# First chunk of a spectral block: the last two tiles' rows placed on chip, the rest read in one transfer, four banks for the first transforms, weight splits spread over three engines

## The chip, the cores and the metric

The kernel runs on one core of a Trainium2 chip. The metric is the device time of one execution in microseconds, here the median of several runs. A core has five engines with queues of their own: TensorE (matmuls and their weight loads), VectorE, ScalarE, GpSimd and SyncE, which here only issues transfers. Each works in program order and waits on semaphores; transfers issued by SyncE, ScalarE or GpSimd run on 16 DMA engines that they share.

## The reference, cut to what matters

The input x has 4096 rows of 640 channels.

```python
mod = (silu(c) @ w_mod).reshape(1, 6, 1, 640)      # sa, ca, ga, sb, cb, gb
h = layernorm(x) * (1 + ca) + sa
x = x + ga * A(h, w1, b1, w2, b2)
h = layernorm(x) * (1 + cb) + sb
x = x + gb * ((silu(h @ w_gate) * (h @ w_up)) @ w_down)
# A: rfft over the 4096 rows; 4 channel blocks of 160; a complex two-layer
# perceptron per frequency (w1, relu, w2); soft shrink by 0.01; inverse rfft
```

All of it is float32 in and out. Where matmuls run on the chip's rounded float32 type, an operand is split into a rounded high part and the remainder, the low part, and the products are summed.

## The kernel before, in words

The 4096 rows are seen as 128 x 32 (n1, n2). **Stage A** (lines 420 to 434) works on eight tiles t, each with four values of n2: `xas[t]` holds 128 partitions (n1) x 4 x 640 channels. Per tile: statistics on VectorE and GpSimd (`ln_stats`), normalisation in place on ScalarE and VectorE (`ln_apply`, L387 and L389), a transform over n1 by five matmul blocks (`dft_a`, L407), and the evacuation of the five banks into the same tile (`evac_a`, L414 to L418). Block i of 0 to 3 takes 128 of 160 channels of each group from row i; block 4 takes the remaining 32 of each group from all four rows (the remainder block). After it, partitions are frequencies. Their order is fixed by the constant `fa`: partition m belongs to a chunk `ch` (0 to 7), and within it to q (4) and jj (4).

The result must be turned so that n2 lies on partitions. It goes through a scratch in device memory, `s1`, in three families: f0 (chunks 0 and 1, every fourth partition, 320 KB per tile), f1 (chunks 2 and 3, 320 KB) and f2 (chunks 4 to 7, every second partition, 640 KB). `write_s1(t, f)` (L338) writes a tile's rows; `load_g(ch)` (L307) reads a chunk into `g`, a tile of 128 partitions (n2, q) x 4 x 640, by four transfers, one for each q. `g` has two buffers. `moves(t)` (L348) is what SyncE issues after tile t: the f0 write always, inputs of later stages, from t=4 f1 and f2 writes of tiles 1 to 3; at t=6 GpSimd is given the read of chunk 0 for n2 below 28, and at t=7 SyncE issues the last four n2, four reads of 40 KB. SyncE's queue then holds the read of chunk 1, `tb` of chunk 1, `b2t`, the f1 writes of tiles 0 and 4 to 7, the read of chunk 2, and the f2 writes of the same tiles (L443 to L453).

**Weights** (`prep_weights`, L253): w1 is split into w1a, w1b and w1c by twelve jobs on ScalarE (high, L280) and VectorE (low, L283) after stage A; w2 into w2a, w2b and w2c by six jobs on GpSimd (high, L278) and VectorE (low).

**Middle stage** (loop at L768): p counts the 32 pairs of chunk and channel group (ch, b), p = 4 ch + b. Its steps: `stage_b` (L542), the transform over n2 into a bank `pb`, and its evacuation, on ScalarE and VectorE, `evac_b` (z, L549 and L550) and `evac_r` (rz, L572 and L582); `stage_l1` (layer 1, L603 to L621, banks p1 and p3), `tail_l1`, `stage_l2` (layer 2, L649, banks p2, evacuated into `tt` on VectorE at L651), `move_x` (tt to `xx` on chip, SyncE, L665), `shrink`, `stage_i` (inverse over n2, L702 to L706, written to the scratch s2 by GpSimd). The order within one p is written out by hand; layer 2 runs one p behind layer 1, `stage_b` one chunk ahead. `stage_b` uses bank b0, or b1 for the remainder block (t=4), one of each. Before the loop, blocks 0, 4, 1 and 2 of chunk 0 are transformed and evacuated, and three low splits of w2 are made; the other three come at the end of p=0. `mods` and `sums` spread the loads and sums of w_mod over the loop; their buffer `wm` (L477) is single, a load waits for the sum before.

After the loop the last chunk's inverse, the first rows of the second normalisation, and then the feed-forward part, from about 330 us to the end.

Memory: the eight tiles `xas` (10,240 bytes per partition each) are released by `stx.close()`, and the pool `p2` takes their place. A tile of p2 may be written once every reader of the tile that lay there is done, scratch writes included. From the allocation: w2a, w2b and w2c lie on xa1, xa2 and xa3, `tt` on xa4, acc, cl, wx and bx on xa0, xx from xa5 on.

Of the kernel before, what the change touches and what calls it, by code (L numbers as in the profile page):

```python
# [6 lines left out]
F32 = mybir.dt.float32  # L7
# [39 lines left out]
def constants():  # L47
# [9 lines left out]
    for ch in range(8):  # L57
        for p in range(2):
            for ri in range(2):
                for jj in range(4):  # L60
                    r = 4 * (2 * p + ri) + jj
                    m = 4 * (16 * (ch % 2) + r) + (0, 2, 1, 3)[ch // 2]
# [109 lines left out]
def body(tc, x, w1, b1, w2, b2, wg, wu, wd, c, wm, k_fa, k_tb, k_tx, k_bm, k_bx, k_ga, k_ge, k_id, out, dbg=None):  # L172
# [9 lines left out]
    s1 = [nc.dram_tensor(f"s1{f}", (n, N2, D), F32, kind="Internal").ap() for f, n in enumerate((32, 32, 64))]  # L182
# [17 lines left out]
    with ExitStack() as top:  # L200
# [33 lines left out]
        with ExitStack() as af:  # L234
# [50 lines left out]

            af.enter_context(tc.manual_schedule())
# [12 lines left out]
            def load_g(ch, lo=0, hi=32, dma=None):  # L299
                if ch < 4:  # L300
                    src = s1[ch // 2].rearrange("(c q j) n d -> c q n j d", c=2, q=4)[ch % 2]
                else:
                    src = s1[2].rearrange("(c q j f) n d -> f c q n j d", c=2, q=4, f=2)[ch // 2 - 2, ch % 2]
                if lo == 0:
                    gs[ch] = fx.tile([P, 4, D], F32, tag="gx", bufs=2, name=f"g{ch}")
                for q in range(4):
                    (dma or nc.sync).dma_start(gs[ch][4 * lo + q:4 * hi:4], src[q, lo:hi])  # L307
# [16 lines left out]
            with tc.tile_pool(name="sp", bufs=1) as sp:  # L324
# [23 lines left out]
                def moves(t):  # L348
                    write_s1(t, 0)
                    if t == 0:  # L350
                        load_x(6)
                        nc.sync.dma_start(c5, c)
                    elif t == 1:
                        load_x(7)
                        raws[1] = load_weights(sp, w1, "1")
                    elif t == 2:
                        nc.sync.dma_start(wm1, wm[:, 1])
                    elif t == 3:
                        load_tb(0)
                        nc.sync.dma_start(b1m, b1[:, 0:8].rearrange("p (r b) -> p r b", r=2))  # L360
                        nc.sync.dma_start(b1r, b1[0:64, 8:12])
                        raws[2] = load_weights(rp, w2, "2")
                    elif t < 7:
                        if t == 6:
                            load_g(0, 0, 28, pool)
                        for f in (1, 2):
                            write_s1(t - 3, f)
                    else:
                        load_g(0, 28, 32)
# [30 lines left out]
                def dft_a(t):  # L400

                    xnr = xas[t].rearrange("p a (b e) -> p a b e", b=NB)
                    for i in range(5):
                        j = 5 * t + i
                        pa = (bank0(j // 4, [P, 512], f"pa{t}_{i}") if j % 4 == 0
                              else ps.tile([P, 512], F32, tag=f"p{j % 4}", name=f"pa{t}_{i}"))
                        mm(pa, fa, xnr[:, i, :, 0:128] if i < 4 else xnr[:, :, :, 128:160], start=True, stop=True)  # L407
                        pas[t, i] = pa

                def evac_a(t):  # L410
                    xa = xas[t]
                    for i in range(5):
# [10 lines left out]
                for t in range(8):  # L423
                    if t + 2 < 8:
                        ln_stats(t + 2)
                    if t + 1 < 8:
                        ln_apply(t + 1)
                    dft_a(t)
                    if t == 7:
                        first_scale()  # L430
                    evac_a(t)
                    if t == 2:
                        act.activation(sc, c5, AF.Silu)
                    moves(t)
# [4 lines left out]
                for job in prep_weights(raws[1], w1a, w1b, w1c, True):  # L439
                    weights_high(*job)  # L440
                    weights_low(*job)

            hp = af.enter_context(tc.tile_pool(name="hp", bufs=1, reuse_waits="tile"))  # L443
            load_g(1)
            load_tb(1)
            b2t = hp.tile([P, 2, NB, BS], F32, name="b2t")
            nc.sync.dma_start(b2t, b2.rearrange("r b o -> (r b o)").partition_broadcast(P))
            for t in (0, 4, 5, 6, 7):
                write_s1(t, 1)
            load_g(2)  # L450
            load_tb(2)
            for t in (0, 4, 5, 6, 7):
                write_s1(t, 2)  # L453
# [4 lines left out]
            pool.dma_start(bm.rearrange("p a b c -> p (a b c)"), k_bm)  # L458
            p2 = af.enter_context(tc.tile_pool(name="p2", bufs=1, side="right", reuse_waits="tile"))

            acc = p2.tile([P, D], F32, name="acc")
            cl = p2.tile([P, D], F32, name="cl")
            wx = p2.tile([P, P], F32, name="wx")
            bx = p2.tile([P, 2, 128], F32, name="bx")
            w2a = p2.tile([P, NB, 640], F32R, name="w2a")
            w2b = p2.tile([P, NB, 640], F32R, name="w2b")
            w2c = p2.tile([P, NB, 640], F32R, name="w2c")
            prep2 = prep_weights(raws[2], w2a, w2b, w2c, False)
            for job in prep2:
# [6 lines left out]
            def mod_load(m, k):  # L476
                wmts[m, k] = p2.tile([P, D], F32, tag="wm", bufs=1, name=f"wm{m}_{k}")  # L477
# [59 lines left out]
            def stage_b(ch, t):  # L537
                g, tb = gs[ch], tbs[ch]
                pb = bank0(1 if t == 4 else 0, [P, 2, 256], f"pb{ch}_{t}")
# [228 lines left out]
            for p in range(LAST + 1):  # L768
# [20 lines left out]
                on(stage_l2, p - 1)  # L789
# [4 lines left out]
                if b == 0 and ch:  # L794
                    for i in range(4):
                        move_x(ch - 1, i)
                if p == 0:
                    for job in prep2[3:]:
                        weights_low(*job)
# [12 lines left out]
            def load_first():  # L812
                x2 = fx.tile([P, 4, D], F32, tag="gx", bufs=2, name="x2_0")
                nc.sync.dma_start(x2, xv[:, 0:4, :])
# [6 lines left out]
            for p in range(LAST + 1, NP):  # L821
# [6 lines left out]
                elif p == LAST + 2:  # L828
                    load_first()
# [3 lines left out]
                on(shrink_low, p - 5)  # L833
            on(shrink, LAST - 1)
# [49 lines left out]
            def first_norm(i):  # L884
                mv, rs, nm = fst[i]
                xn = p2.tile([P, D], F32, tag="co" if i < 2 else "wm", bufs=2 if i < 2 else 1, name=f"xn0_{i}")
# [348 lines left out]
```

## Time and profile before

| | us |
|---|---|
| median of 3 runs (1500.94 to 1502.04) | 1501.2 |
| the profiled execution, its own time | 1502.37 |
| its span, first to last instruction | 1500.6 |
| TensorE busy | 1456.5 (97%) |
| VectorE, ScalarE, GpSimd busy | 871.8, 587.7, 117.0 |
| TensorE busy in 0 to 20, 20 to 40, 40 to 60, 60 to 80, 80 to 100 us | 11.54, 18.09, 10.41, 13.26, 17.50 |

The profile names an instruction by its source line, its engine, and the tiles that it writes and reads (out<-in); for each group it gives the busy time and the idle time just before it, with what ended that idle time. A row like "SPq" or "POOLq" is the queue that issues transfers. "Landing" is when a transfer's last byte is confirmed. The chain of waits runs back from the last instruction of the execution: at each step to what released it, or to the instruction before it.

### The profile page before, as it was taken

What the parts mean: (1) busy time and instruction counts of PE and PEld (TensorE: products, weight loads), DVE (VectorE), ACT (ScalarE), POOL (GpSimd) and SP (SyncE); (2) the same over time, 40 slices, a digit from 0 to 9 for tenths busy, and PEclk for the clock granted to TensorE, in tenths of its full rate; (3) what the DMA queues carried; (4) which work ended last, traced back from release to release, by engine and by line L of the source; (5) the groups of instructions that cost most, each with busy time, mean ns of one, the idle gap of its engine ahead of it and who ended that gap; (6) DMA issues with size and microseconds to landing.
All of it is one profiled execution on the core that took longest, in us unless ns stands there. A gap on an engine that the chain in (4) does not pass through costs nothing.

```text
span 1500.6 us, 20793 instructions
## 1 busy us (share of the span) xinstructions
PE 1456.5 (97%) x8114; PEld 1292.2 (86%) x8114; DVE 871.8 (58%) x1598; ACT 587.7 (39%) x1034; POOL 117.0 (8%) x215
## 2 busy tenths in 40 slices
PE   7599999989999999999999999999999999999998
PEld 2399999868989898989898989898889988898888
DVE  8478888877475437543844374447444744564433
ACT  7569989746232314231323132313231322223220
POOL 5400100030010001000100010001000100000000
PEclk9799999999999999999999999999999999999999
DMA  9946556647432423241324132513241324223210
GB/s 377 319 168 188 167 160 184 206 135 233 140 88 84 111 74 97 85 138 47 100 84 138 53 102 75 154 36 102 80 140 53 94 80 131 62 71 89 70 44 35
DMA packets 183057, 179.92 MB, mean 120 GB/s; under 512 B 19312, under 2 KB 153648, under 8 KB 180016
## 3 DMA queue, kind: packets, MB, share of 16 engines
q1 hardware_dynamic: 173728, 152.56, 34.0%
q0 software_dynamic: 3904, 14.91, 3.0%
q10 hardware_dynamic: 5328, 11.14, 2.0%
q8 instruction: 63, 1.03, 0.3%
q14 instruction: 34, 0.28, 0.1%
HBM read 137.95 MB, written 31.46 MB: 113 GB/s over the span
## 4 chain that ended last, share of the span: by engine, by line
PE 84%; DVE 5%; ACT 4%; DMA 4%; POOL 1%; SPq 1%; issue 1%; DVEq 0%; ACTq 0%; POOLq 0%
PE pd L1143 26%; PE pg L1050 8%; PE pg L1049 8%; PE pg L1051 8%; PE pu L1050 8%; PE pu L1049 8%; PE pu L1051 8%; PE pc L649 1%; PE pl L603 1%; PE pa L407 1%; DMA xx<-tt 1%; PE pb L542 1%; PE pt L1031 1%; DMA s<-xa 1%; DMA g<-s 1%
## 5 line engine op out<-in xcount | busy, mean ns | idle before, releaser
L1143 PE MATMUL pd<-wdh,ah 128*128 128x320 f32 x1664 | 384.4, 310 | 0.1
L1143 PEld LDWEIGHTS pd<-wdh,ah 128*128 128x128 f32 x1664 | 282.4, 188 | 1.0 <-DVE yo L1147 0.4
L1143 PE MATMUL pd<-wdl,ah 128*128 128x320 f32 x832 | 257.0, 309 | 0.0
L1044 DVE TENSOR_TENSOR wl<-wr,wh 128x640 fp32r<-128x640 f32 x216 | 177.5, 822 | 121.5 <-ACT wh L1043 121.5
L1050 PE MATMUL pg<-ht,wh 128*128 128x512 f32 x555 | 216.2, 389 | 0.0
L1049 PE MATMUL pg<-ht,wh 128*128 128x512 f32 x555 | 216.1, 389 | 0.0
L1051 PE MATMUL pg<-ht,wl 128*128 128x512 f32 x555 | 216.0, 389 | 0.0
L1049 PE MATMUL pu<-ht,wh 128*128 128x512 f32 x515 | 200.8, 390 | 0.0
L1050 PE MATMUL pu<-ht,wh 128*128 128x512 f32 x515 | 200.6, 390 | 0.0
L1051 PE MATMUL pu<-ht,wl 128*128 128x512 f32 x515 | 200.4, 389 | 0.0
L1107 ACT ACTIVATE sg<-pg 128x512 f32<-128x512 f32 x104 | 62.2, 598 | 336.2 <-PE pg L1051 335.3
L1120 ACT ACTIVATE ah<-sg 128x512 fp32r<-128x512 f32 x104 | 65.8, 632 | 295.4 <-DVE sg L1119 295.4
L1043 ACT ACTIVATE wh<-wr 128x640 fp32r<-128x640 f32 x216 | 157.1, 728 | 41.5 <-DVE x L1148 38.2
L1147 DVE TENSOR_TENSOR yo<-pd,gbb 128x320 f32<-128x320 f32 x128 | 62.7, 490 | 183.7 <-PE pd L1143 183.7
L1143 PEld LDWEIGHTS pd<-wdl,ah 128*128 128x128 f32 x832 | 156.3, 188 | 0.6
L1051 PEld LDWEIGHTS pg<-ht,wl 128*128 128x128 f32 x555 | 104.2, 188 | 21.8
L1119 DVE TENSOR_TENSOR sg<-pu,sg 128x512 f32<-128x512 f32 x104 | 71.7, 689 | 88.1 <-PE pu L1051 88.1
L1049 PEld LDWEIGHTS pg<-ht,wh 128*128 128x128 f32 x555 | 104.2, 188 | 21.0
L1050 PEld LDWEIGHTS pg<-ht,wh 128*128 128x128 f32 x555 | 104.2, 188 | 21.0
L1121 DVE TENSOR_TENSOR ah<-sg,ah 128x512 fp32r<-128x512 f32 x104 | 72.2, 694 | 72.7 <-ACT ah L1120 72.7
L1051 PEld LDWEIGHTS pu<-ht,wl 128*128 128x128 f32 x515 | 96.7, 188 | 20.3
L1049 PEld LDWEIGHTS pu<-ht,wh 128*128 128x128 f32 x515 | 96.7, 188 | 19.6
(209 smaller groups left out, 2001.6 us busy)
## 6 DMA issues: line engine op xcount, KB each, us to landing
wr<-in_B_w_gate_dram SPq DMA_DIRECT2D x104, 320.0 KB, 3.3
wr<-in_B_w_up_dram SPq DMA_DIRECT2D x104, 320.0 KB, 3.2
x<-in_A_x_dram SPq DMA_DIRECT2D x8, 1280.0 KB, 6.2
out_dram<-x ACTq DMA_DIRECT2D x31, 320.0 KB, 2.2
g<-s SPq DMA_DIRECT2D x28, 320.0 KB, 7.1
xx<-tt SPq DMA_DIRECT2D x56, 160.0 KB, 3.7
s<-co POOLq DMA_DIRECT2D x28, 320.0 KB, 3.4
cr<-s SPq DMA_DIRECT2D x28, 320.0 KB, 3.3
```

The source lines that it names most:

```text
L407: mm(pa, fa, xnr[:, i, :, 0:128] if i < 4 else xnr[:, :, :, 128:160], start=True, stop=True)
L1043: act.activation(wh, wr, AF.Copy)
L1044: dve.tensor_tensor(wl, wr, f32(wh), op=OP.subtract)
L1049: mm(pp, wh[:, k, :], ht[:, k, 0, :], start=(k == 0), stop=False)
L1050: mm(pp, wh[:, k, :], ht[:, k, 1, :], start=False, stop=False)
L1051: mm(pp, wl[:, k, :], ht[:, k, 0, :], start=False, stop=(k == 4))
L1107: act.activation(sg, pg, AF.Silu)
L1119: dve.tensor_tensor(sg, pu, sg, op=OP.mult)
L1120: act.activation(ah[:, 0, :], sg, AF.Copy)
L1121: dve.tensor_tensor(ah[:, 1, :], sg, f32(ah[:, 0, :]), op=OP.subtract)
L1143: mm(pd[:, :320], l, m, start=(i == 0), stop=(i == len(seq) - 1))
L1147: dve.tensor_tensor(yo, pd[:, :320], gbb[:, e], op=OP.mult)
```

## The change

- The order of partitions after stage A (`fa`) is changed so that chunk 0's rows are every eighth partition, and the scratch s1 is laid out with n2 outermost. A scratch write then consists of pieces of one row (2560 bytes) where it was 10,240; a chunk is one read of 128 partitions where it was four of 32.
- `load_g(0, 24)`: at t=5 SyncE issues one read for n2 below 24 (tiles 0 to 5). Tiles 6 and 7 don't pass through the scratch for chunk 0: `place(t)` copies the 16 rows of each n2 from `xas[t]` straight into four partitions of `g`, one transfer of 40 KB for each of the four n2, ahead of that tile's f0 write, which chunk 1 still needs.
- From tile 2 on the remainder block goes first in the matmuls and in the evacuation.
- The f1 and f2 writes: tile 0 at t=4; tile 1 ahead of the read of chunk 1, tile 2 behind it, tiles 3 to 7 behind b2t, then the read of chunk 2.
- Chunk 0's first four transforms take four banks (b0, b1, p2, p3) one after the other, and the evacuations follow.
- w1c is split by GpSimd alone at t=6 (`weights_rest`). Of w2's high splits GpSimd keeps the two of w2a, and ScalarE makes the four of w2b and w2c behind the first evacuations. The low splits of w2 come three at the end of p=0 and three at the end of p=1.
- Layer 2 of block 0 moves from p=1 to p=2, that of blocks 1 and 2 to p=3.
- In p2, w2a, w2b and w2c come first and so lie on xa0, xa1 and xa2; acc, cl, wx and bx on xa3, tt on xa3 and xa4. `wm` gets two buffers, `wx` is padded; p2 then has the size of the eight tiles.
- The load of bm moves from before the GpSimd splits to the end of p=0. The load of x2 at the end of the middle stage is issued by ScalarE, at the end of its step, where SyncE issued it earlier in that step.

```diff
-    s1 = [nc.dram_tensor(f"s1{f}", (n, N2, D), F32, kind="Internal").ap() for f, n in enumerate((32, 32, 64))]
+    s1 = [nc.dram_tensor(f"s1{f}", (N2, n, D), F32, kind="Internal").ap() for f, n in enumerate((32, 32, 64))]
...
+            def weights_rest(rr, wc):
+                pool.tensor_scalar(rr[:, 0], rr[:, 0], sgn[:, 0:1], None, op0=OP.mult)
+                for o in range(2):
+                    for oh, ol, n, src in [(128 * o, 256 + 128 * o, 128, 0), (512 + 32 * o, 576 + 32 * o, 32, 128)]:
+                        v = rr[:, o, :, src:src + n]
+                        pool.tensor_copy(wc[:, :, oh:oh + n], v)
+                        pool.tensor_tensor(wc[:, :, ol:ol + n], v, f32(wc[:, :, oh:oh + n]), op=OP.subtract)
...
+            def load_g(ch, hi=32):
+                f, n = (0, 2) if ch < 2 else (1, 2) if ch < 4 else (2, 4)
+                form = "n (q j e) d -> e (n q) j d" if f == 0 else "n (q e j) d -> e (n q) j d"
+                src = s1[f].rearrange(form, e=n, q=4)[(ch, ch - 2, ch - 4)[f]]
+                gs[ch] = fx.tile([P, 4, D], F32, tag="gx", bufs=2, name=f"g{ch}")
+                nc.sync.dma_start(gs[ch][0:4 * hi], src[0:4 * hi])
...
                 def write_s1(t, f):
-                    nc.sync.dma_start(s1[f][:, 4 * t:4 * t + 4, :], xas[t][(0, 2, 1)[f]:128:(4, 4, 2)[f]])
+                    nc.sync.dma_start(s1[f][4 * t:4 * t + 4].rearrange("n r d -> r n d"),
+                                      xas[t][(0, 2, 1)[f]:128:(4, 4, 2)[f]])
+
+                def place(t):
+                    for i in range(4):
+                        n = 4 * t + i
+                        nc.sync.dma_start(gs[0][4 * n:4 * n + 4], xas[t][0:128:8, i])
...
                 def moves(t):
+                    if t > 5:
+                        place(t)
                     write_s1(t, 0)
...
-                    elif t < 7:
-                        if t == 6:
-                            load_g(0, 0, 28, pool)
+                    elif t == 4:
                         for f in (1, 2):
-                            write_s1(t - 3, f)
-                    else:
-                        load_g(0, 28, 32)
+                            write_s1(0, f)
+                    elif t == 5:
+                        load_g(0, 24)
...
+            for f in (1, 2):
+                write_s1(1, f)
             load_g(1)
             load_tb(1)
+            for f in (1, 2):
+                write_s1(2, f)
             b2t = hp.tile([P, 2, NB, BS], F32, name="b2t")
             nc.sync.dma_start(b2t, b2.rearrange("r b o -> (r b o)").partition_broadcast(P))
-            for t in (0, 4, 5, 6, 7):
-                write_s1(t, 1)
+            for t in (3, 4, 5, 6, 7):
+                for f in (1, 2):
+                    write_s1(t, f)
             load_g(2)
             load_tb(2)
-            for t in (0, 4, 5, 6, 7):
-                write_s1(t, 2)
             stx.close()
...
-            for job in prep2:
+            for job in prep2[0::3]:
                 weights_high(*job, pool)
...
+            for b, tag in ((0, "b0"), (4, "b1"), (1, "p2"), (2, "p3")):
+                stage_b(0, b, tag)
             for b in range(3):
-                stage_b(0, b)
-                if b == 0:
-                    stage_b(0, 4)
                 evac_b(0, b)
                 evac_r(0, b)
-            for job in prep2[:3]:
-                weights_low(*job)
+            for job in prep2[1::3] + prep2[2::3]:
+                weights_high(*job)
...
-                on(stage_l2, p - 1)
+                for b2 in {0: (), 1: (), 2: (0,), 3: (1, 2)}.get(p, (p - 1,)):
+                    on(stage_l2, b2)
...
+                if p < 2:
+                    for job in prep2[p::2]:
+                        weights_low(*job)
                 if p == 0:
-                    for job in prep2[3:]:
-                        weights_low(*job)
+                    pool.dma_start(bm.rearrange("p a b c -> p (a b c)"), k_bm)
...
-            def load_first():
+            def load_first(q):
...
+                if p == LAST + 2:
+                    load_first(nc.scalar)
```

More of the change, by code (lines that the diff above doesn't have):

```diff
@@ L402, in dft_a @@
                     xnr = xas[t].rearrange("p a (b e) -> p a b e", b=NB)
-                    for i in range(5):
-                        j = 5 * t + i
+                    for n, i in enumerate((0, 1, 2, 3, 4) if t < 2 else (4, 0, 1, 2, 3)):
+                        j = 5 * t + n
                         pa = (bank0(j // 4, [P, 512], f"pa{t}_{i}") if j % 4 == 0
@@ L411, in evac_a @@
                     xa = xas[t]
-                    for i in range(5):
+                    for i in (0, 1, 2, 3, 4) if t < 2 else (4, 0, 1, 2, 3):
                         if t == 7 and i % 2:
@@ L433, in body @@
                         act.activation(sc, c5, AF.Silu)
+                    if t == 6:
+                        weights_rest(raws[1][1], w1c)
                     moves(t)
@@ L467, in body @@
             w2c = p2.tile([P, NB, 640], F32R, name="w2c")
+            acc = p2.tile([P, D], F32, name="acc")
+            cl = p2.tile([P, D], F32, name="cl")
+            wx = p2.tile([P, 3 * P], F32, name="wx")[:, 0:P]
+            bx = p2.tile([P, 2, 128], F32, name="bx")
             prep2 = prep_weights(raws[2], w2a, w2b, w2c, False)
-            for job in prep2:
+            for job in prep2[0::3]:
                 weights_high(*job, pool)
@@ L476, in mod_load @@
             def mod_load(m, k):
-                wmts[m, k] = p2.tile([P, D], F32, tag="wm", bufs=1, name=f"wm{m}_{k}")
+                wmts[m, k] = p2.tile([P, D], F32, tag="wm", bufs=2, name=f"wm{m}_{k}")
                 nc.sync.dma_start(wmts[m, k], wm[:, m, k, :])
@@ L535, in width, with stage_b @@
                 return 258 if ch == CE else 256
-            def stage_b(ch, t):
+            def stage_b(ch, t, tag=None):
                 g, tb = gs[ch], tbs[ch]
-                pb = bank0(1 if t == 4 else 0, [P, 2, 256], f"pb{ch}_{t}")
+                pb = ps.tile([P, 2, 256], F32, tag=tag or ("b1" if t == 4 else "b0"),
+                             bufs=2 if tag and tag[0] == "p" else 1, name=f"pb{ch}_{t}")
                 col = slice(128 * t, 128 * t + 128)
```

30 lines of the change are left out of this document (8 added, 22 removed).

## The prediction

> **What bounds the kernel now.** I read first the page's engine rows by slice (1 and 2), then the chain that ended last, then the stretches around the hole.
>
> ```profile
> PE   7599999989999999999999999999999999999998
> PEclk9799999999999999999999999999999999999999
> ```
>
> Forty slices of 37.5 us. TensorE is full from the third slice to the end; the only loose time is in the first two, before 75 us. From 330 us on it is the feed-forward part, 97% TensorE, which the change does not touch. So a gain in the first 100 us moves the end by as much, if the middle stage stays as full as it is.
>
> ```profile
> 50.82 4.74 DMA s<-xa
> 55.58 0.79 SPq L307
> 57.76 7.16 DMA g<-s
> 65.05 3.66 PE pb L542 x16
> 81.44 8.30 DMA s<-xa
> 90.42 2.62 PE pc L649 x16
> 98.79 1.90 PE pl L603 x16
> ```
>
> Start, duration, what ended last (neighbours left out). The last tile's rows go to the scratch (4.74), SyncE then issues four 40-KB reads, the last of them lands 7.16 later, and only then does TensorE start its second transform. 81.44 is a scratch write that VectorE's first tt tile waits for: tt lies where xa4 lay.
>
> ```profile
> 52.00:54.00 2.00, 0.00 (x0) 0.00 (x0) 2.00 (x7) 2.00 (x6) 0.66 (x1) 0.50 0.66 277
> 60.00:62.00 2.00, 0.00 (x0) 0.00 (x0) 0.00 (x0) 0.00 (x0) 2.00 (x2) 0.50 1.28 263
> 66.00:68.00 2.00, 2.00 (x12) 2.00 (x11) 0.15 (x1) 0.69 (x1) 1.73 (x3) 0.50 1.06 419
> ```
>
> Stretch, then busy time of TensorE, its weight loads, VectorE, ScalarE and GpSimd, the granted clock, DMA share and GB/s. All three compute engines stand still; DMA is busy at a low rate (263 GB/s against 419 in 30 to 48 us).
>
> ```profile
> 89.87 0.89 DVE L651 TENSOR_TENSOR tt<-pc,b2t 128x320 f32<-128x320 f32 x2 [2.69 <-DMA s<-xa]
> ```
>
> The second stall: 2.69 us.
>
> **Stage A, new order.** Tile t's remainder block goes first and needs all four normalised rows; before, row 0 was enough. The evacuation gains nothing: the remainder's evacuation overwrites columns that every row's matmul reads, so ScalarE still starts after the fifth block. ScalarE is 17.99 of 18 us busy in 30 to 48 us, so what it waits is lost. Five blocks are 4.43 us (17.74 us for four tiles). Tile 4 started at 31.44 on its first row, whose second ScalarE row ended at 32.20; with the same effect in tiles 2 and 3 (0.6) tile 4 starts at 32.85, tile 5 at 37.65 and ends at 42.1, its evacuation (2.6) at 44.7, tile 7's rows (2.5) at 47.2, its five blocks at 51.65, its evacuation (1.55) at 53.2: **2.4 us later** than 50.79. Lower bound 0, upper 3.
>
> **The scratch and the read.** SyncE's queue after tile 5: its f0 write issues at 44.7 (before 43.54) and lands after 4.3 us (these writes took 4.1 to 5.9 from issue); the read of rows n<24 waits for it, so it issues at 49.1. 983 KB in 2560-byte pieces: 2.9 us (the row-wise x loads, same pieces, moved 317 GB/s in 4 to 8 us, 383 in 8 to 12) plus the 2.1 that a small transfer takes anyway (the lone 160-KB xx move landed in 2.4): 54.1. Behind it stand tile 6's four 40-KB placements (0.6 each, row g<-s L307), its write, and tile 7's four; the rows of tile 7 are ready at 52.85. The trace never shows more than eight SyncE transfers unfinished (the x load issued at 9.21 waited for that of 3.05 to land at 9.19), so tile 7's third placement waits for the big read: 54.1, the fourth at 54.8, landed 2.4 later. **TensorE's second transform can start at 57.2 instead of 64.9.** A placement is not in the trace. Low end 1.8 us (a small write at 312 landed in 1.81), high end 7.16 (the 40-KB reads above); I take 2.4, since an xx move is also SBUF to SBUF in 2560-byte pieces.
>
> **Splits of w1.** The w1c part leaves ScalarE (2.06 us) and VectorE (2.06) for GpSimd: one scale of 1.88 (w2c<-rr,sgn) and four copies and four subtracts, about 7.1 by GpSimd's 1.81 per 128x640 and 0.86 per 128x320. GpSimd was idle from 41.1 to 53.3, so 41 to 50 hides it; without that cover w1c would still have until 63. Eight remaining jobs end at 56.5, ahead of 57.2.
>
> **First blocks.** Before: 65.05 to 73.28 for four blocks, with pauses for bank b0. Now four banks take them at once: at half clock 1.83 each (3.66 for two), at full clock 0.9; with the clock up at about 62, done at 63.4. Then ScalarE is the limit: z 0.69 and rz 0.95 for three blocks, last done at 65.6. Behind them stand two w2b and two w2c high splits (0.73 each by L686 and L1043): six GpSimd jobs of 1.81 became two there and four here. w2b overwrites xa1, whose writes are long in. w2c overwrites xa2, whose last write is queued behind the read of chunk 1: issue 60.1, landing 67.6 after chunk 1 (3.9), tb (0.7) and the row writes (0.9 and 1.7 for 320 and 640 KB). So ScalarE is free for layer 1 at **69.1**, a stall of 0.5. Behind these splits wait the evacuations of layer 1's first block, hence both p1 banks, hence TensorE's second block.
>
> **From there to layer 1 of block 4.** VectorE per block: h 0.76, u 0.48, z 0.75, r 0.42, rz 0.98, 3.4 in all, plus three low splits of 0.82 to 0.88, 2.5, in p=0 and in p=1. p=0 ends at 76.8, p=1 at 82.7; layer 2 of block 0 can start at 81.5 (its last low split is used last). From then TensorE sets the pace: layer 2 three times 2.4, layer 1 2.5, a transform 0.9, 10.6 in all: layer 1 of block 4 at **92.1; before it was 98.62**. Layer 2 put off by one step costs nothing here, since tt is used only by the first move to xx after block 3. tt lies on xa3 and xa4 now; their last write lands by 74.5, so the stall of 2.69 goes. Gain **6.5 us**.
>
> **Clock.** The granted clock fell to 0.50 at 51.4 and was full at 68.4, half again from 71.9 to 75.3 after an idle of 1.7. The Trainium skill, TensorE: Matmul & The Clock Gate, Part 1, says that the gate judges free-running windows of about 3.4 us; by it the idle of TensorE before its second layer-1 block would halve that block too, 1.2 us more on the path, and the sum would be 5.3. The trace's half window agrees with the rule; I leave it out of the sum, since VectorE is the limit there; 5.3 lies inside the forecast's range.
>
> **The rest.** All scratch writes turn into 2560-byte pieces; the feed-forward's output rows, same pieces, keep near the 10-KB rate, so I price it at 0 to +1 us, off the path by the eight us that f1 and f2 writes have. Chunks 2 to 7 are read in one DMA instead of four; 1.8 us of SyncE issue each, hidden, since they are asked for a chunk ahead. Second wm buffer: VectorE waited once, 0.6; counted 0 to -0.6. bm moved behind p=0: used at p=7, 0. x2 issued from ScalarE, some 8 us later: 0.5 of issue on an engine with idle of 2 us there, landing (8.0 at 290.5) by 308, used at 317: 0; if not covered, +0.5.
>
> **Sum.** The profiled execution took 1502.37 us (span 1500.6, 1.8 around it); minus 6.5 is 1495.9. The runs' median, 1501.2, is 1.2 below it: **1494.7**.
>
> **Rivals.**
> - *Late rows.* Placements as slow as the 40-KB reads: 7.16 instead of 2.4, 4.8 later on the path, gain 1.7: 1499.5. For: small transfers with four partitions, seen once and slow. Against: those shared the engines with GpSimd's reads (215 to 265 GB/s then), these come behind one read. The Trainium skill, DMA: Bandwidth & Descriptors, Rules for kernel authors, advises merging transfers under 64 KB; eight of 40 KB go against it, and here the trace's 7.16 agrees with it. Chance 0.13.
> - *Better.* ScalarE's and VectorE's queue doesn't bind, and TensorE keeps the old distance: 33.7 us from landing to layer 1 of block 4, less the 2.7 stall, 31.0: 88.2, gain 10.4, 1490.8. Chance 0.15.
> - *Slower: the w2c splits on ScalarE.* They hold the queue until xa2's f2 write lands. Each us past 67.1 costs one; at 74 the gain is gone, and above 77 the kernel is over 0.2% slower, 1504.5 at 77.5. For: it is in-order, and nothing covers it. Against: that needs 14 to 17 us from issue to landing; the longest of these writes took 9.0. Chance 0.06.
> - *Doesn't arrive.* TensorE starts early, but ScalarE (27.67 of 30) and VectorE (26.61) bind in 120 to 150 us and the gain is swallowed: about 1501. Against: they are fed earlier by as much. Chance 0.05.
> - Forecast: 0.61.
>
> **Numbers.** The forecast's own range is 1492.5 to 1497.5 (start of the second transform plus or minus 1.5, stage A 0 to 3). The range wanted takes in the better case and half of late rows: 1490.8 to 1499.3. A measurement of this kernel tells about 0.2% (3 us) from no change: faster than 1498.2 is forecast, better and a fifth of late rows, 0.79; within, most of late rows, the swallowed gain and part of the forecast's tail, 0.15; slower 0.06.
>
> **What would show it.** Right: TensorE's wait for g ends at 56 to 59; tile 7's evacuation ends about 2 us later; ScalarE's w2c split waits under 2 us for a scratch write; layer 1 of block 4 starts at 90 to 95; no wait of tt for s<-xa; from 100 us the same pattern, shifted. Wrong: placements of over 5 us, a wait of ScalarE of over 5 us at the w2c split, GpSimd's w1c work running past 60, or a shift at 100 us that is not there at 330.

## The result, and the profile after

The changed kernel takes **1505.89 us** (median of 12 runs, 1503.0 to 1510.94) against 1500.55 for the kernel before on the same chip (12 runs, 1497.56 to 1503.52): ratio 1.0036, 95% interval 1.0024 to 1.0048. It is 5.3 us slower where I had forecast 6.5 us faster. The profiled execution took 1509.56 us, span 1507.8; it is 3.7 us above the median, the second slowest of the twelve.

The page's rows by slice, 37.7 us each:

```profile
PE   6679999999999999999999999999999999999998
PEclk9889999999999999999999999999999999999999
```

Everything still happens in the first three slices; the third is now a 7 where it was a 9. From the feed-forward's first matmul to the end of the span it is 1166.7 us in both kernels (1507.8 less 341.13, and 1500.6 less 333.92). So the loss is made before 341 us. ScalarE's first evacuation of layer 1 at block 4 starts at 108.17 where it was 99.83, 8.3 us later, so all of it is made before that.

The chain that ended last, start, duration, what:

```profile
45.27 2.07 ACT xa L432 x4
47.36 5.13 DMA s<-xa
52.51 0.63 SPq L314
54.02 8.42 DMA g<-xa
62.46 4.79 DMA s<-xa
67.31 0.57 SPq L314
67.92 1.59 SPq L305
69.56 1.46 SPq L346
71.06 7.70 DMA s<-xa
78.84 1.45 ACT w2c L281 x2
93.10 2.32 PE pc L669 x14
102.97 4.15 PE pc L669 x16
```

Tile 5's write is issued at 47.36, not 44.7. The read behind it is issued at 52.51. A row sent on chip right behind it (g<-xa, issued at 54.02) takes 8.42 us to land, and only then is tile 7's f0 write issued (62.46). SyncE's queue goes on from there: the read of chunk 1 (67.31), `tb` of chunk 1 (67.92), tile 2's writes (69.56 and 71.06). The one that begins at 71.06 is the scratch write for which ScalarE's split of w2c waits; it lands at 78.8, where the forecast had 67.6. So the chain runs through SyncE's queue and not through TensorE's second transform. That transform is late as well, and the two come together at ScalarE: its evacuations and the w2b split are done at 77.39, 1.45 us before w2c's place is free. At 102.97 begins a layer-2 step that takes 4.15 us instead of 2.35. TensorE and ScalarE one after the other, with the idle time ahead of a group and what ended it in brackets:

```profile
66.85 6.45 PE L562 MATMUL pb<-tb,g 128*128 128x128 f32 x32 [10.54 <-DMA s<-xa]
81.21 1.01 PE L623 MATMUL pl<-z,w1a 128*128 128x256 f32 x3 [4.54 <-ACT h L627]
93.10 0.41 PE L669 MATMUL pc<-w2a,h 128*128 128x320 f32 x1 [1.39 <-DVE w2a L284]
102.97 1.07 PE L669 MATMUL pc<-w2a,h 128*128 128x320 f32 x3 [1.81 <-DVE tt L671]
```

ScalarE of the same kernel, in the same columns, at the time of TensorE's wait of 4.54:

```profile
76.03 1.36 ACT L281 ACTIVATE w2b<-rm 128x640 fp32r<-128x640 f32 x2
78.84 0.83 ACT L281 ACTIVATE w2c<-rr,sgn 128x640 fp32r<-128x640 f32 x1 [1.45 <-DMA s<-xa]
79.58 0.72 ACT L281 ACTIVATE w2c<-rr 128x640 fp32r<-128x640 f32 x1
80.32 0.47 ACT L626 ACTIVATE h<-pl,b1m 128x256 f32<-128x256 f32 x1
```

The first 10.54 is put down to a scratch write; but what TensorE reads there is g, and the last of its rows landed at about 66.8, so it is the wait for that row. The 4.54 is new: TensorE has finished layer 1 of block 0 at 75.8 and one more transform at 76.7, and can't go on, because ScalarE splits w2 from 76.03 to 80.3 before it evacuates that block. The 1.81 is new too. The old stall of tt is gone, as forecast (first tt at 96.97, no wait in front of it).

### The profile page after: what moved, and what is told of

The parts are those of the page before. It is cut to its first block, busy times and chain, and to the rows that moved or that the text cites. A ratio compares the mean times of both kernels' runs of the same rounds, so it can differ in the third digit from the quotient of the medians.

```text
span 1507.8 us, 20743 instructions
## 1 busy us (share of the span) xinstructions
PE 1459.9 (97%) x8114; PEld 1295.1 (86%) x8114; DVE 872.9 (58%) x1594; ACT 588.7 (39%) x1034; POOL 115.5 (8%) x216
## 4 chain that ended last, share of the span: by engine, by line
PE 86%; DVE 5%; ACT 3%; DMA 3%; SPq 1%; issue 1%; POOL 0%; DVEq 0%; ACTq 0%
PE pd L1165 26%; PE pg L1072 8%; PE pg L1071 8%; PE pg L1073 8%; PE pu L1072 8%; PE pu L1071 8%; PE pu L1073 8%; PE pc L669 3%; PE pl L623 2%; DMA s<-xa 1%; PE pt L1053 1%; PE pb L562 1%; DMA xx<-tt 1%; PE pa L421 1%; DVE st_a L192 1%
## 5 line engine op out<-in xcount | busy, mean ns | idle before, releaser
L1073 PEld LDWEIGHTS pu<-ht,wl 128*128 128x128 f32 x515 | 96.7, 188 | 20.2
L1071 PEld LDWEIGHTS pu<-ht,wh 128*128 128x128 f32 x515 | 96.7, 188 | 19.6
```

The lines of the kernel that those rows point to most:

```text
L1071: mm(pp, wh[:, k, :], ht[:, k, 0, :], start=(k == 0), stop=False)
L1073: mm(pp, wl[:, k, :], ht[:, k, 0, :], start=False, stop=(k == 4))
```

## The experiments

All run times are medians of 6 to 12 executions, taken beside the kernel before on the same chip (its median there 1501.3 to 1501.5). The changed kernel's row is from the result, where the kernel before had 1500.55, so gains over it are given by the medians and are somewhat larger by the ratios. Three legs are read from each run's trace: **T0**, the start of the second transform; **leg 2**, from there to ScalarE's first evacuation of layer 1; **leg 3**, from there to that evacuation for block 4, after which the pattern is steady. One profile is one execution, and T0 moves by some 3 us between executions of nearly the same front part (66.85 and 63.57 in after and e4), so the legs say where, and the medians say how much.

| | median, us | ratio to before | T0 | leg 2 | leg 3 |
|---|---|---|---|---|---|
| before | 1501.3 | | 65.05 | 9.98 | 24.80 |
| after | 1505.89 | 1.0036 [1.0024, 1.0048] | 66.85 | 13.47 | 27.85 |
| e1_order_only | 1503.15 | 1.0011 [1.0000, 1.0021] | 67.18 | 9.46 | 25.27 |
| e2_old_order | 1503.14 | 1.0016 [1.0004, 1.0028] | 64.34 | 12.39 | 28.30 |
| e3_all_scratch | 1506.41 | 1.0035 [1.0023, 1.0047] | 63.20 | 11.91 | 26.31 |
| e4_l2_early | 1502.94 | 1.0010 [1.0001, 1.0019] | 63.57 | 13.31 | 24.36 |
| e5_both_undone | 1500.16 | 0.9993 [0.9984, 1.0003] | 61.31 | 12.38 | 24.34 |
| e6_split_read | 1501.64 | 1.0004 [0.9994, 1.0014] | 62.91 | 12.32 | 24.34 |
| e7_four_banks | 1501.29 | 0.9997 [0.9987, 1.0007] | 65.97 | 8.97 | 25.01 |
| e8_split_no_place | 1499.61 | 0.9990 [0.9982, 0.9999] | 61.03 | 11.91 | 24.35 |
| e9_highs_gpsimd | 1500.21 | 0.9991 [0.9980, 1.0002] | 64.74 | 9.18 | 28.40 |
| e10_split_highs | 1496.67 | 0.9968 [0.9954, 0.9981] | 61.24 | 8.38 | 24.45 |
| e11_tile2_early | 1496.83 | 0.9973 [0.9963, 0.9984] | 61.48 | 8.74 | 24.34 |
| e12_two_reads | **1494.84** | 0.9960 [0.9946, 0.9975] | 59.22 | 8.74 | 24.37 |
| e13_three_undone | 1496.20 | 0.9970 [0.9960, 0.9980] | 61.38 | 9.17 | 24.41 |
| e14_scalar_highs | 1503.49 | 1.0016 [1.0007, 1.0024] | 65.39 | 12.19 | 22.58 |
| e15_l2_and_highs | 1497.72 | 0.9974 [0.9965, 0.9982] | 65.08 | 8.72 | 24.52 |
| e16_w1c_back | 1496.80 | 0.9971 [0.9960, 0.9981] | 61.49 | 9.18 | 24.33 |

My first theory: the order of the remainder block, and layer 2 put off, each cost some us, and the rows sent on chip bring little. Rivals: each of the three is free, as forecast.

**e1**, the kernel before with the remainder block first from tile 2 on (matmuls and evacuation), and **e2**, the changed kernel with the old order of the matmuls:

```diff
-                    for i in range(5):
-                        j = 5 * t + i
+                    for n, i in enumerate((0, 1, 2, 3, 4) if t < 2 else (4, 0, 1, 2, 3)):
+                        j = 5 * t + n
...
-                    for i in range(5):
+                    for i in (0, 1, 2, 3, 4) if t < 2 else (4, 0, 1, 2, 3):
```

```diff
-                    for n, i in enumerate((0, 1, 2, 3, 4) if t < 2 else (4, 0, 1, 2, 3)):
+                    for n, i in enumerate(range(5)):
```

> The kernel before with one part of the change: from tile 2 on the remainder block goes first in the matmuls and in the evacuation. Theory 1 (the order starves TensorE and so delays stage A): tile 7's evacuation ends 3 to 5 us later than 50.8, the first transform of chunk 0 starts that much later than 65.05, and the time is 3 to 5 us over before, 1503.6 to 1505.6. Theory 2 (the order is hidden; stage A's delay in the changed kernel comes from its transfers): the time stays within 1 us of before.

> The changed kernel with the matmul blocks of stage A in the old order 0 to 4 (the evacuation still takes the remainder first). Theory 1 (order): tile 7's evacuation ends near 51 to 52 in place of 55.9, the first transform of chunk 0 starts 3 to 5 us before 66.85, and the time falls by 3 to 5 us, to 1501 to 1503. Theory 2 (transfers): the start of the first transform stays within 1 us of 66.85, since SyncE's queue sets it, and the time within 1 us of 1505.9.

The order alone costs 1.7 us on the kernel before, between the two theories and at the edge of what the interval tells (1.0000 to 1.0021). Undoing it in the changed kernel takes 2.8 us away. Stage A ends at 54.93 in e1 and at 51.04 in e2. Why stage A ends later than the forecast 2.4 us, the granted clock shows for the larger part. TensorE of the changed kernel, from its wait in tile 2 on:

```profile
23.32 10.52 PE L421 MATMUL pa<-xa,fa 128*128 128x512 f32 x20 [2.36 <-DVE xa L401]
```

The same group in e3 (below), which has the same order:

```profile
22.14 8.82 PE L421 MATMUL pa<-xa,fa 128*128 128x512 f32 x20 [2.38 <-DVE xa L401]
```

The changed kernel by stretches: length, busy time of TensorE, its weight loads, VectorE, ScalarE, GpSimd, the granted clock, DMA share and GB/s:

```profile
24.00:26.00 2.00, 2.00 (x4) 0.88 (x4) 2.00 (x6) 1.58 (x3) 0.47 (x3) 0.65 1.03 435
26.00:28.00 2.00, 2.00 (x3) 0.67 (x2) 2.00 (x9) 1.20 (x2) 1.10 (x2) 0.50 1.03 399
```

Both wait 2.4 us for the fourth row of tile 2, which only the new order needs so early. In the changed kernel the clock is then halved from 24.6 to 28.0, and twenty matmuls take 10.52 instead of 8.82; in e3 it isn't, and stage A ends at 53.09, the 53.2 of the forecast almost to the digit. Of the 2.9 us between the two ends (55.97 and 53.09) the clock makes 1.7; the other 1.2 is the group's later start (23.32 against 22.14), for which no run shows the reason. Of the six profiles with the new order, five have that half window, none of those with the old order has one in stage A.

**e3**, the changed kernel with nothing sent on chip: chunk 0 is read whole after tile 7's write.

```diff
-                    if t > 5:
-                        place(t)
...
-                        load_g(0, 24)
+                        pass
+                    elif t == 7:
+                        load_g(0)
```

> The changed kernel without the placements on chip: chunk 0 is read whole from the scratch, in one transfer issued after tile 7's f0 write. Theory 1 (the read and the placements queued behind it are slow, so the on-chip way brings little): the first transform starts at 65 to 69, within 2 us of 66.85, and the time is within 2 us of 1505.9. Theory 2 (placements do what they are for; the loss is elsewhere): the first transform starts 6 us later or more (write to landing 4.7, then a read of 6 to 8), and the time rises by 5 us or more, to over 1511.

The median is that of the changed kernel: sending the rows brings nothing that shows, though the whole read waits for the last write of all. (T0, at 63.20, came before both theories' ranges; this profile is of e3's fastest execution.)

**e4**, the changed kernel with layer 2 one p behind layer 1 as before, and all six low splits of w2 at the end of p=0:

```diff
-                for b2 in {0: (), 1: (), 2: (0,), 3: (1, 2)}.get(p, (p - 1,)):
+                for b2 in (p - 1,):
...
-                if p < 2:
-                    for job in prep2[p::2]:
+                if p == 0:
+                    for job in prep2:
```

> The changed kernel with layer 2 one step behind layer 1 from the start again, and all six low splits of w2 at the end of p=0. Theory 1 (two layer-2 steps in one p wait for the two p2 banks, and the clock halves): no wait of layer 2 for tt near 103, layer 1 of block 4 starts 2 to 4 us earlier than 106.96, and the time falls by 2 to 4 us, to 1502 to 1504. Theory 2 (VectorE is the limit, so the order of layer 2 doesn't matter): the time stays within 1 us of 1505.9.

1502.94: 3 us below the changed kernel. Leg 3 is 24.36 against 27.85, and 24.3 to 24.5 in every later run with this edit, against 26.3 to 28.4 in every run with layer 2 put off. Two layer-2 steps in p=3 need four banks, and p2 has two: the second step waits 1.81 for VectorE to empty one, and where the clock then drops (half from 103.1 to 106.5) the step itself takes 4.15 instead of 2.35. In e3 the clock held there, and its leg 3 of 26.31 is the wait, shown here, and little more:

```profile
97.77 0.71 PE L669 MATMUL pc<-w2a,h 128*128 128x320 f32 x3 [1.81 <-DVE tt L671]
```

e4 also moves three low splits of w2 from p=1 to p=0; that the banks are the cause rests on this wait.

**e5**, both undone (the edits of e2 and e4), and **e6**, which is e5 with the read of chunk 0 cut: n below 16 at t=4, 16 to 24 where the one read was (`load_g` gets a lower bound for it, left out here).

> The changed kernel with the old order of the remainder block's matmul (first, as in the kernel before, evacuation still remainder first) and with layer 2 back at one block's distance and all six low halves of w2 before it, both at once. Theory 1 (two separate costs, one in stage A and one in the first blocks): 1505.9 less 3.0 less 3.9, so about 1499, a ratio of 0.998 to 1.000 against the kernel before. Rival (both costs stand on one stretch of the path, so that taking away the second brings little): 1502 to 1503, as either edit alone gave.

```diff
                     elif t == 4:
+                        load_g(0, 0, 16)
...
-                        load_g(0, 24)
+                        load_g(0, 16, 24)
```

> As e5_both_undone, with the read of the scratch for chunk 0 cut in two: n below 16 as soon as tile 3's rows have landed (at tile 4's end), n 16 to 24 where the one read was. Theory 1 (the one read of 983 KB took 7.5 us and the sent rows of tiles 6 and 7 queued behind it, which is where the forecast gain went): the last rows land 3 to 5 us sooner, the first transform starts at 59 to 61 instead of 63.6 to 66.9, and the time is 3 to 4 us below e5_both_undone. Rival (layer 1 waits for weights and for ScalarE, not for the rows): the transform starts sooner, layer 1 does not, and the time is that of e5_both_undone within 1 us.

e5 bears out that the two costs are separate. e6 was a miss: T0 did not move forward, and the time is 1.5 us above e5, outside both theories. SyncE stood until 52.4 waiting for tile 5's write, which had queued behind the early read and the two writes of tile 0, and then had ten transfers to issue at 0.6 us each; the last row left at 58.4.

**e7**, the kernel before with four banks for chunk 0's first transforms (`stage_b` gets the bank as an argument, left out here), and **e8**, e6 without rows sent on chip (a third read, n 24 to 32, after tile 7's write):

```diff
+            for b, tag in ((0, "b0"), (4, "b1"), (1, "p2"), (2, "p3")):
+                stage_b(0, b, tag)
             for b in range(3):
-                stage_b(0, b)
-                if b == 0:
-                    stage_b(0, 4)
                 evac_b(0, b)
```

```diff
-                    if t > 5:
-                        place(t)
...
                         load_g(0, 16, 24)
+                    elif t == 7:
+                        load_g(0, 24, 32)
```

> The kernel before with four banks for chunk 0's first transforms alone. Theory 1 (the transforms end 2.0 us sooner, as they did in the trace of the changed kernel, 6.2 us in place of 8.2, and layer 1 follows them): 1 to 2 us faster than before, ratio 0.9987 to 0.9993. Rival (ScalarE's evacuations and the split of the weights hold layer 1, not the transforms): 0, ratio 0.9997 to 1.0003.

> As e6_split_read, but nothing is sent on chip: n 24 to 32 of chunk 0 come through the scratch, in one read after tile 7's write. Theory 1 (with the big read out of the way, sending the rows on chip saves the write's 4.8 us before the last read): 3 to 5 us above e6_split_read. Rival (the sent rows cost as much on their queue as the write and the read, as in the run without them): within 1 us of e6_split_read.

The four banks alone bring nothing that can be told (0.9987 to 1.0007). e8 is 2 us faster than e6, against both theories: from the end of SyncE's wait on, four issues lead to the last read where e6 has ten to its last row, and that read (4.3 us) took no longer to land than the rows. By then T0 was 4 us ahead of before and the gain 1 to 2 us, so the rest had to be lost behind T0. Its place shows in leg 2, 11.9 to 13.5 in every run that has ScalarE split w2b and w2c. So **e9** is the changed kernel with those high halves back on GpSimd and nothing else, **e10** is e8 with them:

```diff
             for job in prep2[1::3] + prep2[2::3]:
-                weights_high(*job)
+                weights_high(*job, pool)
```

> The changed kernel with the high halves of w2b and w2c back on GpSimd, nothing else. Theory 1 (ScalarE's 2.8 us for them and its wait of 1.45 us for tile 2's write stand ahead of layer 1's first evacuation, so the rival that I had given little is part of the loss): layer 1 is evacuated 3 to 4 us sooner after the first transform and the time is 2 to 4 us below the changed kernel, 1502 to 1504. Rival (the low halves on VectorE and layer 2's wait at the third block take the same time back): within 1 us of the changed kernel, 1505 to 1507.

> As e8_split_no_place, with the high halves of w2b and w2c on GpSimd. Theory 1 (as for e9_highs_gpsimd: ScalarE holds layer 1 by 3.5 us, 70.2 to 73.7 in the trace of e5_both_undone): 2 to 4 us below e8_split_no_place, 1496 to 1498, faster than the kernel before by 0.2 to 0.35%. Rival (layer 2 waits for the low halves on VectorE, which now wait for GpSimd): within 1 us of e8_split_no_place.

e9 takes 5.7 us off the changed kernel, more than theory 1 gave it and more than any other part undone alone; leg 2 falls from 13.47 to 9.18, which places 4.3 of them. e10 takes 2.9 off e8. ScalarE of e13 (below), which has the same edit, at the same place as the rows above:

```profile
69.58 0.95 ACT L592 ACTIVATE rz<-pb,ca 32x256 fp32r<-32x256 f32 x2 [0.33 <-DVE rz L602]
70.55 0.47 ACT L626 ACTIVATE h<-pl,b1m 128x256 f32<-128x256 f32 x1
```

The evacuation of layer 1 follows the last rz at once, and TensorE's wait of 4.54 is gone.

**e11**, tile 2's two writes ahead of chunk 1's read, and **e12**, in addition chunk 0 in two reads, n below 16 at t=5 and the rest after tile 7's write, so that SyncE doesn't stand at the wait for tile 5's write:

```diff
             for f in (1, 2):
                 write_s1(1, f)
+            for f in (1, 2):
+                write_s1(2, f)
             load_g(1)
             load_tb(1)
-            for f in (1, 2):
-                write_s1(2, f)
```

```diff
-                        load_g(0, 0, 16)
...
-                        load_g(0, 16, 24)
+                        load_g(0, 0, 16)
...
-                        load_g(0, 24, 32)
+                        load_g(0, 16, 32)
```

> As e10_split_highs, with tile 2's two writes to the scratch issued ahead of chunk 1's read, so that w2c's place comes free some 5 us sooner. Theory 1 (GpSimd's w2c waits for that write, and VectorE's low halves and layer 2 of the first block for GpSimd): 1 to 2 us below e10_split_highs. Rival (chunk 1's read, some 2.5 us later, delays its first transforms by as much): the same within 0.5 us.

> As e11_tile2_early, with chunk 0 read in two pieces that never hold SyncE's queue on a write just issued: n below 16 at tile 5's end, the rest after tile 7's write. Theory 1 (SyncE's stand at the wait for tile 5's row, to 51.0 in the trace of e8_split_no_place with stage A over at 50.2, delays the last writes): the first transform starts 1 to 2 us sooner, and the time is 1 us lower. Rival (the last read is twice as large and takes that back): the same or 1 us more.

e11 changes nothing. e12 starts the second transform at 59.22 and takes **1494.84 us**, 0.25 to 0.54% faster than the kernel before. It is the lowest median here, but its interval overlaps those of e10, e11, e13 and e16. The rows by slice on its page:

```profile
PE   6699999999999999999999999999999999999998
```

The undone edits alone take back 2.8, 3.0 and 5.7 us, 11.5 of a loss of 5.3 (3.0, 3.9 and 6.8 by the ratios). Four more runs ask whether they add up and what is left. **e13** undoes all three; **e14** puts ScalarE's splits alone into the kernel before; **e15** undoes layer 2 and ScalarE's splits; **e16** is e13 with w1c split by ScalarE and VectorE as before. The edits of e14 and e16 (the others are those above):

```diff
-            for job in prep2:
+            for job in prep2[0::3]:
                 weights_high(*job, pool)
...
+            for job in prep2[1::3] + prep2[2::3]:
+                weights_high(*job)
             for job in prep2[:3]:
                 weights_low(*job)
```

```diff
-                    if t == 6:
-                        weights_rest(raws[1][1], w1c)
...
-                    if job[0] is not w1c:
-                        weights_high(*job)
-                        weights_low(*job)
+                    weights_high(*job)
+                    weights_low(*job)
```

> The changed kernel with all three undone: the old order of the remainder's matmul, layer 2 at one block's distance with the low halves before it, and the high halves of w2b and w2c on GpSimd. What is left of the change is the rows sent on chip, the one read, the four banks, the split of w1c on GpSimd and the tail. Theory 1 (the separate gains share a stretch, and ScalarE's 3 us come on top of e5_both_undone's 1500.2): 1496.5 to 1498. Rival (they add up, 1505.9 less 3.0, 3.9 and 5.4): 1493 to 1494.5, close to my forecast of the whole change.

> The kernel before with the high halves of w2b and w2c on ScalarE behind the first evacuations, as in the changed kernel, nothing else. Theory 1 (ScalarE's 2.8 us, and its wait for the writes whose place w2c takes, stand ahead of layer 1): 2 to 5 us slower than before, a ratio of 1.0013 to 1.0033. Rival (in the kernel before, layer 2's first result waits for a write to the scratch until 89.87 anyway, which covers it): ratio 0.9995 to 1.0008.

> The changed kernel with layer 2 at one block's distance (low halves before it) and the high halves on GpSimd, the new order of the remainder kept. Theory 1 (two layer-2 steps in one pass wait for one pair of banks, whoever splits the weights): 2.5 to 4 us below e9_highs_gpsimd, 1496 to 1498. Rival (with ScalarE free the deferral costs nothing, as forecast): within 1 us of e9_highs_gpsimd's 1500.2.

> As e13_three_undone, with w1c's halves split by ScalarE and VectorE at the end of stage A, as in the kernel before, in place of GpSimd. Theory 1 (ScalarE and VectorE wait 9 to 10 us for the first transform after that work, so it is covered either way): within 0.7 us of e13_three_undone. Rival (ScalarE's longer list of splits holds up the sent rows' queue): 1 to 2 us above e13_three_undone.

e13 lands at 1496.20, just under theory 1's range and 1.7 us above the rival's: the three together are worth 9.7 us, less than the 11.5 of their separate gains. That they share a stretch is likely but not shown: the 1.8 us between rest on five medians, each known to about 1.5 us. One way down the table: splits on GpSimd 5.7, then layer 2 back 2.5, then the old order 1.5. e15 shows that layer 2's delay costs 2.5 us with ScalarE free as well. e16 bears out that w1c's split is hidden wherever it is done. e14 is 2.2 us slower than before; its one profile shows the 2.2 in leg 2 (12.19 against 9.98) but given back in leg 3 (22.58), so why the median is slower is not shown by it.

## Why the prediction was wrong, point by point

Two terms of the sum failed: the start of the second transform at 57.2 (the read and the rows behind it were taken too fast, and a halved clock in stage A was left out), and layer 2's delay, put at nothing. A third, ScalarE's splits of w2 ahead of layer 1, stood in the sum at nearly its size, but it was the dearest part of the change to keep (5.7 us by e9). The forecast had ScalarE's evacuation of layer 1 at block 4 start at 93.3 (TensorE at 92.1, and 1.2 from there, as in both traces); it came at 108.17. The 14.9 us between them split over the three legs: T0 at 66.85 where I had 57.2 (9.65), leg 2 13.47 for 11.9 (1.6), leg 3 27.85 for 24.2 (3.65). Between the medians the miss is 11.2 us (1505.89 for 1494.7), 3.7 fewer than in this profile's execution, which is that much above its median.

- *Stage A, new order: plus 2.4.* The mechanism was right and e3 hits it (53.09). Left out was that a wait of 2.4 us can halve the clock for 3.4 us. That and the later start of the group put tile 5's write 2.66 late and the end of tile 7 at 55.97. I had weighed the clock gate only for the second layer-1 block.
- *The scratch and the read: mis-sized, the largest term.* Write of tile 5: 5.13 to land for 4.3. The one read of 983 KB: 7.5 us for 5.0. By stretches, the changed kernel, columns as above:

```profile
54.00:56.00 2.00, 1.31 (x10) 0.96 (x9) 1.31 (x2) 1.61 (x4) 1.93 (x4) 1.00 0.96 228
56.00:58.00 2.00, 0.32 (x3) 0.23 (x3) 1.65 (x5) 2.00 (x6) 0.63 (x1) 1.00 1.08 231
62.00:64.00 2.00, 0.00 (x0) 0.00 (x0) 0.00 (x0) 0.00 (x0) 0.00 (x0) 0.50 0.38 127
```

  The DMA engines are full at 228 to 231 GB/s, where I had counted 317 to 383 from the loads of x. I had the lower rate in view, 263 GB/s in the same place of the kernel before, and put it down to small reads beside GpSimd's; one read of 96 partitions has it too. Behind the read the slot limit that I had named bit harder: tile 7's third row waited for the read (issue 60.01), the fourth (issue 61.76) for the *first row sent*, issued at 53.23 behind the read and out some 8.5 us. The fourth then landed in 5.0, not 2.4. With the late write: 3.4 (issue of the read), 2.5 (its length), 1.05 (the slot), 2.65 (the landing), the 9.6 of T0.
- *Late rows, the rival at 1499.5.* Right about the rows (5.0 to 8.5 us) but for the reason that speaks against it in my text: "these come behind one read" is what made them late. The Trainium skill, DMA: Bandwidth & Descriptors, Rules for kernel authors, tells to coalesce transfers under 64 KB. e8 against e6 points the same way, one read of 320 KB (1499.61) for eight rows of 40 KB (1501.64); e12 against e13 (1494.84, 1496.20) is not clear of noise.
- *First blocks: four banks done at 63.4.* Right in form (6.2 us for four blocks against 8.2), worth nothing that e7 can tell.
- *ScalarE free 11.9 us after T0.* Leg 2 is 11.91 in e3 and e8, where w2c has no wait, and 13.47 in the changed kernel with its wait of 1.45 for w2c's place, which I had at 0.5. The duration was right. What failed is what it was compared with: I wrote that VectorE's queue is the limit after it, and so saw no alternative to 11.9; with the splits on GpSimd and four banks leg 2 is 8.4 to 9.2, and leg 3 (layer 2 at one p) the same 24.4. So ScalarE's splits are on the path: 3 to 4 us of leg 2, by the medians 2.2 (e14), 2.9 (e10) and, in the changed kernel as it stands, 5.7.
- *Slower: the w2c splits on ScalarE, chance 0.06.* The rival named the place, and its condition came true: xa2's last write landed at 78.8 for 67.6, not by a slow write (7.7 us) but because SyncE's queue was late (read of chunk 1 issued at 67.31 for 60.1) and slow behind it (11.5 us to that landing for 7.5). By its rule, one us for each past 74, that gives 1506, the measured time. This agreement is in part luck: ScalarE stood only 1.45 us for the write, as T0 was late by the same queue, and the rest came from the splits themselves and from layer 2. What tile 2's writes ahead of chunk 1's read bring while ScalarE has the splits was not run; e11 has them with GpSimd.
- *Clock, left out of the sum.* It did halve there (79.2 to 86.0), and leaving it out was right: leg 3 is 24.35 in e8, with the clock at half from 73.2 to 80.1, and 24.45 in e10, where it held.
- *"Layer 2 put off by one step costs nothing here."* Wrong: 2.5 to 3 us. I asked who uses tt, not which banks the two steps in p=3 need.
- *tt's stall goes; w1c hidden; the rest 0.* Right: no wait at the first tt, e16 within 0.7 us of e13, the same 1166.7 us from 341 us on.

What remains of the change once the three edits are out, 0.30% or 4.5 us (0.9960 to 0.9980), is a real gain, mostly in T0 (61.38 for 65.05); it is the forecast's direction at two thirds of its size.

## What to carry to other kernels

Ahead of the first full pass, work moved from an idle engine onto one that evacuates must be priced by what queues behind it, even where that engine is idle on average; here GpSimd's slow splits (1.81 us each) cost nothing that shows, ScalarE's fast ones (0.73) cost 2 to 6 us in all. For each step that is put off, count the banks that it needs together with its new neighbour, not only the first use of its result. A transfer that is small is not early: here rows of 40 KB took 8.4 us behind a read of 983 KB, and each cost its 0.6 us of issue and one of the eight places for unfinished transfers.

## What the runs showed of the hardware that I had not expected

- **The read of chunk 0 from the scratch ran at little over half the rate.** Pieces of 2560 bytes took 172 to 191 ns on average in the big read (from the DMA share and GB/s of the rows at 54 and 56) and 102 in the median in loads of x (8 to 12 us) and in writes (44 to 48 us); the DMA engines moved 228 to 262 GB/s for 6 us against 399 to 435 in 24 to 28 us. In e12 a read of 655 KB took 6.0 us from issue to landing, at 195 to 251 GB/s for three of them. Why, and whether reads of other chunks are as slow, is not shown.
- **A wait of the same length halves the clock in one execution and not in the next.** 2.36 us at tile 2 gave a half window from 24.6 to 28.0, 2.38 in e3 gave none. The Trainium skill, TensorE: Matmul & The Clock Gate, Part 1, says that the gate's window of 3413 ns runs freely; the windows here are 3.4 long and agree. Counted in such windows from each trace's changes of clock, the phase explains both pairs: the changed kernel has 2.1 us of the wait at tile 2 in one window (21.2 to 24.6) and the whole 1.81 in another (99.7 to 103.1), and each is followed by half clock; in e3 a boundary at 21.6 cuts the first wait into 1.8 and 0.5, one at 96.7 the second into 0.7 and 1.1, and the clock held. How much idle time in one window suffices is known no better than that it is about 1.8. A half window cost 1.7 us at tile 2, and so may be part of the 3 us or so by which executions of one kernel differ.
